# Splitting evacuations from matmuls in a hand-ordered attention and wave-mixing kernel, with a named PSUM bank for each result and a new order of all steps

## The chip, the cores and the metric

The kernel runs on one core of a Trainium2 chip. The metric is device time in microseconds of one execution: the median of three runs. One execution was profiled, and all views of the profile shown here are of that one.

## The reference

Two layers, one after the other, for a batch of 8. The attention of each of 8 heads is a sum of two: full attention among positions pooled by four (576 positions become 144), repeated four times, and a local attention in which a position sees only those less than four away. The second layer takes the result as x (576 rows of 512), makes phases, mixes the rows with two token weights and then the channels.

```
q_d, k_d, v_d = mean of each 4 positions of q, k, v
out_up = repeat(softmax(q_d k_d^T / 8) v_d, 4)
out_local = softmax(where(|i - j| < 4, q k^T / 8, -1e9)) v
x = (out_up + out_local), heads side by side           # 8 x 576 x 512

theta = x @ w_theta
y = w_tok_r @ (x * cos(theta)) + w_tok_i @ (x * sin(theta))
u = x + y
out = u + max(u @ w_ch, 0)
```

Inputs and output are float32; the kernel computes in bfloat16 with float32 sums.

## The kernel before

The work of one batch is cut into steps, and the program is one string, `ORDER`, in which each letter stands for the next step of one kind (a Python generator per letter; batch 0 first, then batch 1, and so on). `pin()` ties every instruction to the one before it on its engine, so the string fixes the order of each engine's queue: an instruction that waits holds up all behind it on that engine. Different engines run as far ahead of one another as data and buffers let them.

The steps of one batch, with their letters before the change:

- L (13 steps): loads on SP's queue into 15 staging buffers of `stg`; eight k and q tiles of two heads each (288 KB), alternating k and q, then five v tiles in two halves. A load waits for the cast of the tile that had its buffer, 15 tiles earlier.
- C (13): casts to bfloat16 into `k_tm`, `q_tm`, `v_w`: POOL, but for batch 0 ACT (k) and DVE (q).
- A (4): nine transposes on PE into a pair of banks (`pstr`, L267), then ACT's copy to `kT` or `qT` (L268).
- a (4): sums of four positions: `kd` on DVE (L281), `qdT` on POOL (L290, L291; batch 0 on DVE, L285).
- U, u: pooled v on PE, ACT's copies, and POOL's products into `vd` (L317).
- P (2): pooled scores in tiles of 64 rows and 128 columns (`psSd`, L339) with ACT's exp; S (3): local scores in blocks of 64 (`psS`, L375) with ACT's exp (L382); M (3): the band mask on DVE.
- N (2): pooled outputs (`psnd`, L403, L409), normalised on DVE; n: their transposes and DVE's copy `xdT`; V (5): local outputs (`psloc`, L447), DVE's reciprocal `rl` and product `tmp`.
- T (5): transposes of `tmp` by matmul, with DVE's sum with the pooled part into `xT` (L480, L485).
- H (5): phases `psth` (L501), ACT's sin and cos into `cs` (L506, L507); the fifth is the tail of 64 rows (`pstt`). h: DVE's product `zT` of the tail and its DMA transpose into row group 8 of `z` (L524, L527). Z (4): transposes of `xT` (L537) and DVE's products `z` (L538).
- X (8): the token mix, nine matmuls of 288 columns each (`psu`, L558) and DVE's sum `uT` (L562). All nine row groups of `z` go into each.
- r (5): four DMA transposes of `uT` into `ur` on SP (L571), and POOL's copy of the tail into `ut`; t: the DMA transpose `utr` of two batches' tails.
- R (4), Q: channels (`psr`, L588; `psrt`); O (4), q: DVE's relu and sum `osb`, `osbt` (L607, L613), which need `ur` or `utr`; o, s: stores on SP.

The weights have letters of their own: l (20 loads: four of `w_theta`, twelve of the token weights, four of `w_ch`), c (20 casts on POOL), and w (18): transposes of the token weights (`wps`, L245) into `WT` (L250), nine for each half of 288 token columns. The token weights are cut into rows of 128, 128 and 32 for each half. D (4) is a group of six matmuls on zeros (`wu`, L160), which stands at the end of the string.

In the transposes, scores and other steps with a result in PSUM, the matmuls and the instruction that takes the result out belong to one step. PSUM banks are handed out in turn: `w1` has four single banks, `w2` two pairs. Before the first step, constants are made: DVE's memsets and copies, with POOL's selects between them (`halves_of`, L89 to L99), in the order of the text. So DVE's first casts of q stand behind all of them.

Of the kernel before, what the change touches and what calls it, by code (L numbers as in the profile page):

```python
# [14 lines left out]

P = 128
B = 8
# [10 lines left out]

# [12 lines left out]
OC = [128, 128, 32, 128, 128, 32]  # L41
OR = [0, 128, 256, 288, 416, 544]
# [3 lines left out]
def kernel(  # L46
# [14 lines left out]
    wpool = ctx.enter_context(tc.tile_pool(name="wpool", bufs=1))  # L61
    stg = ctx.enter_context(tc.tile_pool(name="stg", bufs=15))
    work = ctx.enter_context(tc.tile_pool(name="work", bufs=2))
    moep = ctx.enter_context(tc.tile_pool(name="moep", bufs=2))
    ps2 = ctx.enter_context(tc.tile_pool(name="ps2", bufs=1, space=bass.MemoryType.PSUM))
    ps1 = ctx.enter_context(tc.tile_pool(name="ps1", bufs=1, space=bass.MemoryType.PSUM))

    turn2, turn1 = itertools.cycle("ab"), itertools.cycle("abcd")

    def w2(name, dt=FP32):  # L70
        return ps2.tile([P, 2, 512 if dt == FP32 else 1024], dt, tag="w2" + next(turn2), name=name)

    def w1(name, dt=FP32):
        return ps1.tile([P, 512 if dt == FP32 else 1024], dt, tag="w1" + next(turn1), name=name)

    dve, act, gp = nc.vector.tensor_copy, nc.scalar.copy, nc.gpsimd.tensor_copy
# [3 lines left out]
    ident = const.tile([P, P], BF16, name="ident")  # L80
    nc.vector.memset(ident, 0.0)
    nc.gpsimd.affine_select(out=ident, in_=ident, compare_op=ALU.not_equal, fill=1.0,
                            base=0, pattern=[[-1, P]], channel_multiplier=1)
    identw = ident.rearrange("p (g w) -> p g w", w=W)

    pihc = const.tile([P, 1], FP32, name="pihc")
    nc.vector.memset(pihc, PIH)

    def halves_of(t, n, val, cuts):  # L89


        full = work.tile([P, 2, W], BF16, tag="full", name=f"full_{t.name}")
        nc.vector.memset(full, val)
        for g in range(2):
            for base, col, row in cuts[g]:
                nc.gpsimd.affine_select(out=full[:, g, 0:n], in_=full[:, g, 0:n], compare_op=ALU.is_ge, fill=0.0,  # L96
                                        base=base - W * g * row, pattern=[[col, n]], channel_multiplier=row)
        for g in range(2):
            nc.vector.tensor_copy(out=t[W * g:W * g + W, :], in_=full[W * g:W * g + W, g, 0:n])  # L99

    band = const.tile([P, W], BF16, name="band")
    halves_of(band, W, 1.0, [[(3, -1, 1), (3, 1, -1)]] * 2)


    kTs, kds = [], []
    for i in range(2):
        t = const.tile([P, 4, NCH * CH], BF16, name=f"kT{i}")
        nc.vector.memset(t[:, :, S:], 0.0)
        kTs.append(t)
        t = const.tile([P, 4, NCH, KP], BF16, name=f"kd{i}")  # L110
        nc.vector.memset(t, 0.0)
        kds.append(t)

    v_ws = []
    for i in range(2):
        t = const.tile([P, NCH, H, 66], BF16, name=f"v_w{i}")
        nc.vector.memset(t[:, :, :, 64:65], 1.0)
        v_ws.append(t)

    vds = []  # L120
    for i in range(2):
        t = const.tile([P, 2, H, 66], BF16, name=f"vd{i}")
        nc.vector.memset(t[:, :, :, 64:65], 0.0)
        for c in range(4):
            nc.vector.memset(t[KP * c:KP * c + PG, 0, :, 64:65], 1.0)
            nc.vector.memset(t[KP * c:KP * c + SD - 4 * PG, 1, c::4, 64:65], 1.0)
        vds.append(t)

    PU = []
    for c in (0, 1, 4):
        r = const.tile([P, KP], BF16, name=f"pu{c}")
        cuts = []
        for blk in (2 * c, 2 * c + 1):
            lo, n = W0[blk] - CH * c, STEP * blk - W0[blk]
            cuts.append([(lo, -4, 1), (3 - lo, 4, -1)])
            if n:
                cuts[-1].append((-n, 0, 1))
            if n + OWN[blk] < W:  # L140
                cuts[-1].append((n + OWN[blk] - 1, 0, -1))
        halves_of(r, KP, 0.25, cuts)
        PU.append(r)
    PU = [PU[0], PU[1], PU[1], PU[1], PU[2]]

    own = const.tile([P, 4], BF16, name="own")
    nc.vector.memset(own, 1.0)
    nc.gpsimd.affine_select(out=own, in_=own, compare_op=ALU.is_ge, fill=0.0,
                            base=0, pattern=[[-KP, 4]], channel_multiplier=1)
    nc.gpsimd.affine_select(out=own, in_=own, compare_op=ALU.is_ge, fill=0.0,  # L150
                            base=KP - 1, pattern=[[KP, 4]], channel_multiplier=-1)

    warm = const.tile([P, 512], BF16, name="warm")
    nc.vector.memset(warm, 0.0)

    def warm_up():
        for i in range(WARM):
            ps = w1(f"wu{i}")
            for _ in range(6):
                nc.tensor.matmul(out=ps, lhsT=ident, rhs=warm, start=True, stop=True)  # L160
            yield

    WARM = 4
# [5 lines left out]
    def stage(b, key):  # L169
        t = staged[b, key] = stg.tile([P, S], FP32, tag="st", name=f"st{b}_{key}")  # L170
        return t

    def load(b):
        for hh in range(4):
            for nm, src in (("k", k), ("q", q)):
                nc.sync.dma_start(out=stage(b, f"{nm}{hh}"),
                                  in_=src[b, 2 * hh:2 * hh + 2].rearrange("h (p r) d -> (h p) (r d)", r=WR))
                yield
        for c in range(NCH):
            t = stage(b, f"v{c}")[:, 0:DM].rearrange("p (h d) -> p h d", d=D)  # L180
            for g in range(2):
                lo = W0[2 * c + g]
                nc.sync.dma_start(out=t[W * g:W * g + W], in_=v[b, :, lo:lo + W, :].rearrange("h p d -> p h d"))
            yield

    def cast(b):
        q_tm = work.tile([P, 2, WR, 2, D], BF16, tag="q_tm", name=f"q_tm{b}")
        k_tm = work.tile([P, 2, WR, 2, D], BF16, tag="k_tm", name=f"k_tm{b}")
        v_w = v_ws[b % 2]
        inputs[b] = (q_tm, k_tm, v_w)  # L190
        eng = CASTS.get(b, CASTS[None])
        for hh in range(4):
            for i, (nm, dst) in enumerate((("k", k_tm), ("q", q_tm))):
                eng[i](out=dst[:, hh // 2, :, hh % 2, :],  # L194
                       in_=staged.pop((b, f"{nm}{hh}")).rearrange("p (r d) -> p r d", d=D))
                yield
        for c in range(NCH):
            eng[2](out=v_w[:, c, :, 0:D], in_=staged.pop((b, f"v{c}"))[:, 0:DM].rearrange("p (h d) -> p h d", d=D))  # L198
            yield

    CASTS = {0: (act, dve, gp), None: (gp, gp, gp)}
# [3 lines left out]
    wth = wpool.tile([P, 4, DM], BF16, name="wth")  # L205
    wch = wpool.tile([P, 4, DM], BF16, name="wch")
    WT = wpool.tile([P, 9, S], BF16, name="WT")
    w_tm = [moep.tile([P, 6, S], BF16, tag="uT", name=f"wtm{ri}") for ri in range(2)]

    def wide_weight(w, nm):  # L210
        for i in range(4):
            nc.sync.dma_start(out=stage("w", f"{nm}{i}")[:, 0:DM], in_=w[P * i:P * i + P, :])
            yield

    def weight_loads():
        yield from wide_weight(moe_w_theta, "th")
        for hf in range(2):
            for ri, w in enumerate((moe_w_tok_r, moe_w_tok_i)):
                for ct in range(3 * hf, 3 * hf + 3):
                    nc.sync.dma_start(out=stage("w", f"tok{ri}{ct}")[0:OC[ct]], in_=w[OR[ct]:OR[ct] + OC[ct], :])  # L220
                    yield
        yield from wide_weight(moe_w_ch, "ch")

    def weight_casts():
        for i in range(4):
            gp(out=wth[:, i, :], in_=staged.pop(("w", f"th{i}"))[:, 0:DM])
            yield
        for hf in range(2):
            for ri in range(2):
                for ct in range(3 * hf, 3 * hf + 3):  # L230
                    gp(out=w_tm[ri][0:OC[ct], ct, :], in_=staged.pop(("w", f"tok{ri}{ct}"))[0:OC[ct]])
                    yield
        for i in range(4):
            gp(out=wch[:, i, :], in_=staged.pop(("w", f"ch{i}"))[:, 0:DM])
            yield
# [16 lines left out]

    parts = {}

    def turns(b):
        q_tm, k_tm, v_w = inputs[b]
# [4 lines left out]
        for i in range(2):  # L263
            for n, (tm, To) in enumerate(((k_tm, kT), (q_tm, qT))):
# [6 lines left out]
                )  # L271
                yield

    EVAC = (act, act)

    def sums(b):
        qT, kT, qdT, kd = parts[b]
# [424 lines left out]
```

## Time and profile before

| what | value |
|---|---|
| median of 3 runs | 257.98 us (257.93 to 260.31) |
| profiled execution, span | 258.0 us |
| PE busy | 229.7 us, 89% |
| DVE busy | 196.5 us, 76% |
| ACT, POOL busy | 138.9 us, 54%; 118.0 us, 46% |
| mean granted PE clock | 0.980 |
| DMA | 49.85 MB, 193 GB/s in the mean |
| matmuls | 3332 |

The profiled execution has no time of its own beside its span of 258.0 us, which is the median to 0.02 us. Busy times of a queue are unions of its instructions' spans; a matmul that runs at half clock is busy for twice as long. The page's second part cuts the span in 40 slices of 6.45 us. "Waits" put the idle time before an instruction down to what came last. SP runs no arithmetic: its queue issues the DMAs, and the DMA engines work beside all.

### The profile page before, as it was taken

What the parts mean: (1) busy time and instruction counts of PE and PEld (TensorE: products, weight loads), DVE (VectorE), ACT (ScalarE), POOL (GpSimd) and SP (SyncE); (2) the same over time, 40 slices, a digit from 0 to 9 for tenths busy, and PEclk for the clock granted to TensorE, in tenths of its full rate; (3) what the DMA queues carried; (4) which work ended last, traced back from release to release, by engine and by line L of the source; (5) the groups of instructions that cost most, each with busy time, mean ns of one, the idle gap of its engine ahead of it and who ended that gap; (6) DMA issues with size and microseconds to landing.
All of it is one profiled execution on the core that took longest, in us unless ns stands there. A gap on an engine that the chain in (4) does not pass through costs nothing.

```text
span 258.0 us, 8100 instructions
## 1 busy us (share of the span) xinstructions
PE 229.7 (89%) x3332; PEld 157.8 (61%) x3332; DVE 196.5 (76%) x404; ACT 138.9 (54%) x190; POOL 118.0 (46%) x201
## 2 busy tenths in 40 slices
PE   0168879999999998699998999989899899999998
PEld 0154656588557765377676667766586457677633
DVE  4298797878998965487889698897789987856452
ACT  3456469634985579504894568357775765250000
POOL 3664989464796596449274444941043020000000
PEclk9999999589999999979999999999999999999999
DMA  7999996698998995998699864994088316015756
GB/s 228 265 248 357 344 198 175 197 248 202 285 225 194 287 275 135 208 326 151 129 311 259 156 153 103 326 216 62 3 125 241 90 41 185 12 35 122 205 177 231
DMA packets 83173, 49.85 MB, mean 193 GB/s; under 512 B 68160, under 2 KB 68160, under 8 KB 83136
## 3 DMA queue, kind: packets, MB, share of 16 engines
q1 hardware_dynamic: 83136, 49.33, 77.0%
q8 instruction: 26, 0.43, 0.7%
q14 instruction: 11, 0.09, 0.1%
HBM read 34.11 MB, written 9.44 MB: 169 GB/s over the span
## 4 chain that ended last, share of the span: by engine, by line
PE 63%; DVE 12%; DMA 8%; ACT 6%; POOL 6%; issue 4%; SPq 0%; DVEq 0%; POOLq 0%; ACTq 0%
PE psu L558 25%; PE psr L588 7%; PE psth L501 6%; PE pstr L267 6%; DMA z<-zT 4%; PE xTps L480 3%; DVE tmp L456 2%; DMA st_k<-in_k_dram 2%; DVE xT L485 2%; PE wu L160 2%; PE psS L375 2%; PE psxt L537 2%; POOL full_pu L96 2%; PE psnd L403 2%; PE psloc L447 2%
## 5 line engine op out<-in xcount | busy, mean ns | idle before, releaser
L558 PE MATMUL psu<-WT,z 128*128 128x288 bf16 x576 | 81.1, 292 | 4.9 <-DVE z L538 2.4
L558 PEld LDWEIGHTS <-z 128*128 128x128 bf16 x576 | 55.4, 99 | 22.0 <-DVE z L538 2.7
L562 DVE TENSOR_TENSOR uT<-psu,xT 128x288 bf16<-128x288 f32 x64 | 29.0, 454 | 19.9 <-PE psu L558 19.3
L198 POOL CAST v_w<-st_v 128x512 bf16<-128x512 f32 x40 | 26.1, 664 | 30.3 <-DMA st_v<-in_v_dram 16.1
L506 ACT ACTIVATE cs<-psth,pihc 128x512 bf16<-128x512 f32 x32 | 22.2, 694 | 20.9 <-PE psth L501 16.8
L501 PE MATMUL psth<-wth,xT 128*128 128x512 bf16 x128 | 33.2, 387 | 0.2 <-ACT cs L507 0.2
L588 PE MATMUL psr<-wch,uT 128*128 128x512 bf16 x128 | 31.3, 379 | 1.1 <-DVE osbt L613 0.6
L456 DVE TENSOR_TENSOR tmp<-psloc,rl 128x512 bf16<-128x512 f32 x40 | 27.7, 692 | 1.4
L382 ACT ACTIVATE pm<-psS 128x1024 bf16<-128x1024 f32 (+1 forms) x24 | 20.5, 883 | 14.9 <-PE psS L375 14.7
L268 ACT COPY kT<-pstr 128x1152 bf16<-128x1152 bf16 x16 | 18.0, 1126 | 16.3 <-PE pstr L267 16.1
L538 DVE TENSOR_TENSOR z<-psxt,cs 128x1024 bf16<-128x1024 bf16 x32 | 21.5, 684 | 6.2 <-PE psxt L537 3.8
L573 POOL COPY ut<-uT 128x256 bf16<-128x256 bf16 x8 | 3.2, 400 | 50.2 <-DVE uT L562 50.2
L485 DVE TENSOR_TENSOR xT<-xTps,xdT 128x464 bf16<-128x464 f32 (+1 forms) x40 | 24.7, 629 | 1.0 <-PE xTps L480 0.4
L607 DVE SCALAR_TENSOR_TENSOR osb<-psr,ur 128x512 f32<-128x512 f32 x32 | 21.5, 685 | 5.0 <-DMA ur<-uT 3.5
L194 POOL CAST k_tm<-st_k 128x576 bf16<-128x576 f32 x28 | 19.4, 694 | 5.5 <-DMA st_k<-in_k_dram 5.2
L268 ACT COPY qT<-pstr 128x1152 bf16<-128x1152 bf16 x16 | 18.1, 1133 | 7.0 <-PE pstr L267 7.0
L281 DVE TENSOR_REDUCE kd<-kT 128x290 bf16<-128x1160 bf16 x16 | 21.6, 1353 | 0.0
L194 POOL CAST q_tm<-st_q 128x576 bf16<-128x576 f32 x28 | 18.7, 667 | 5.0 <-DMA st_q<-in_q_dram 4.9
L290 POOL TENSOR_TENSOR two<-qT 128x576 f32<-128x576 bf16 x14 | 16.0, 1146 | 7.9 <-ACT qT L268 7.9
L390 DVE TENSOR_TENSOR pm<-pm,band 128x1024 bf16<-128x1024 bf16 (+1 forms) x24 | 18.9, 787 | 1.0 <-ACT pm L382 1.0
L267 PE MATMUL pstr<-ident,k_tm 128*128 128x128 bf16 x144 | 12.1, 236 | 8.4 <-ACT k_tm L194 7.1
L317 POOL TENSOR_TENSOR vd<-last,own 128x256 bf16<-128x256 bf16 x16 | 10.1, 653 | 20.6 <-ACT last L311 20.6
(83 smaller groups left out, 370.0 us busy)
## 6 DMA issues: line engine op xcount, KB each, us to landing
st_v<-in_v_dram SPq DMA_DIRECT2D x80, 128.0 KB, 4.1
st_k<-in_k_dram SPq DMA_DIRECT2D x32, 288.0 KB, 4.5
st_q<-in_q_dram SPq DMA_DIRECT2D x32, 288.0 KB, 5.0
out_dram<-osb SPq DMA_DIRECT2D x32, 256.0 KB, 3.1
stw_tok<-in_moe_w_tok_r_dram SPq DMA_DIRECT2D x4, 288.0 KB, 6.2
stw_tok<-in_moe_w_tok_i_dram SPq DMA_DIRECT2D x4, 288.0 KB, 5.8
stw_th<-in_moe_w_theta_dram SPq DMA_DIRECT2D x4, 256.0 KB, 5.7
stw_ch<-in_moe_w_ch_dram SPq DMA_DIRECT2D x4, 256.0 KB, 5.8
```

What stands on the lines that cost most here:

```text
L194: eng[i](out=dst[:, hh // 2, :, hh % 2, :], in_=staged.pop((b, f"{nm}{hh}")).rearrange("p (r d) -> p r d", d=D))
L198: eng[2](out=v_w[:, c, :, 0:D], in_=staged.pop((b, f"v{c}"))[:, 0:DM].rearrange("p (h d) -> p h d", d=D))
L267: nc.tensor.transpose(out=ps[:, P * r:P * r + P], in_=tm[:, i, r, :, :], identity=ident)
L268: EVAC[n](out=To[:, 2 * i:2 * i + 2, 0:S].rearrange("p a (w r) -> p a w r", r=WR), in_=ps[:, 0:P * WR].rearrange("p (r a w) -> p a w r", a ...
L281: nc.vector.tensor_reduce(out=kd[:, hs, :, 0:PG].rearrange("p e g m -> p (e g) m"), axis=AX.X, op=ALU.add, in_=kT[:, hs, :].rearrange("p e ...
L456: nc.vector.tensor_tensor(out=tmp.rearrange("p g (j d) -> p g j d", d=D), in0=pv[:, :, :, 0:D], in1=rl.unsqueeze(3).to_broadcast([P, 2, 4, ...
L485: nc.vector.tensor_tensor(out=xT[:, :, CH * c:CH * c + cnt].rearrange("p e (m j) -> p e m j", j=4), in0=ps[:, :, 0:cnt].rearrange("p e (m ...
L501: nc.tensor.matmul(out=th, lhsT=xT[:, dc, P * c:P * c + P], rhs=wth[:, dc, :], start=(dc == 0), stop=(dc == 3),)
L506: nc.scalar.activation(out=cs[:, 0, :], in_=th, func=AF.Sin, bias=pihc, scale=1.0)
L558: nc.tensor.matmul(out=ps[:, 0:288], lhsT=z[:, j, P * dc:P * dc + P], rhs=WT[:, j, cols], start=(j == 0), stop=(j == 8),)
L562: nc.vector.tensor_tensor(out=uT[:, dc, cols], in0=ps[:, 0:288], in1=xT[:, dc, cols], op=ALU.add)
L588: nc.tensor.matmul(out=psr, lhsT=uT[:, dc, P * c:P * c + P], rhs=wch[:, dc, :], start=(dc == 0), stop=(dc == 3),)
```

## The change

It rewrites the kernel around the same arithmetic.

- Each step with a PSUM result is split in two, the matmuls and the evacuation, with letters of their own. Where it matters below: A/a (turns and ACT's copies), S/s/m, P/p, N/n, O/o/i (local outputs, reciprocals, products), T/t, H/h, G/g/Z/z (the tail: phases, sines, DVE's product, DMA transpose on SP), X/y, V/v (weight turns and DVE's copies), J/j (mix and `uT`), R/f/F (DMA transposes of `uT`, the tail's copy, `utr`), K/b, E/r (channels and relu), D, Y (stores), d and e (key and query sums), k (constants), L, C, l, c as before, w (a single warm-up matmul, which does not occur in the new order).
- A second string names the PSUM bank of each result, any of eight; `two()` takes the pair that holds it. Tiles are fixed buffers (`rot`), with the same counts as the pools had.
- The k tiles of one pair of heads are loaded and cast next to each other. Batch 0's casts stay on ACT and DVE.
- The token weights are loaded, cast and transposed in six tiles of 96 rows.
- A pooled score of a head pair is two matmuls of 64x64 instead of one of 64 rows and 128 columns.
- The constants are a sequence among the others; those with selects are made on POOL alone.
- The order is new, and the warm-up matmuls at the end are gone.

```
+    def one(dt=FP32):
+        i = int(next(banks))
+        ap = pairs[i // 2][:, i % 2, :]
+        return ap if dt == FP32 else ap.bitcast(dt)
...
-        full = work.tile([P, 2, W], BF16, tag="full", name=f"full_{t.name}")
-        nc.vector.memset(full, val)
+        full = rot("full", [P, 2, W], BF16, 2)
+        nc.gpsimd.memset(full, val)
...
-            nc.vector.tensor_copy(out=t[W * g:W * g + W, :], in_=full[W * g:W * g + W, g, 0:n])
+            nc.gpsimd.tensor_copy(out=t[W * g:W * g + W, :], in_=full[W * g:W * g + W, g, 0:n])
...
+    ITEMS = ["k0", "k1", "q0", "q1", "k2", "k3", "q2", "q3", "v0", "v1", "v2", "v3", "v4"]
+    CASTS = {0: "aavvaavvppppp", None: "ppppppppppppp"}
...
-OC = [128, 128, 32, 128, 128, 32]
-OR = [0, 128, 256, 288, 416, 544]
+OC = 96
...
-            for par in range(2):
-                nc.tensor.matmul(out=dst(par), lhsT=kd[64 * par:64 * par + 64, hh, 0:4, :],
-                                 rhs=qdT[64 * par:64 * par + 64, hh, :], start=True, stop=True)
+            for m in range(2):
+                for par in range(2):
+                    nc.tensor.matmul(out=dst(par)[64 * m:64 * m + 64], lhsT=kd[64 * par:64 * par + 64, hh, 2 * m:2 * m + 2, :],
+                                     rhs=qdT[64 * par:64 * par + 64, hh, :], start=True, stop=True)
...
     def mix(b):
...
+        z = zs[b]
+        for dc, hf in pieces(b):
+            ps = held["u", b, dc, hf] = one()[:, 0:288]
+            for j in range(9):
+                nc.tensor.matmul(out=ps, lhsT=z[:, j, P * dc:P * dc + P], rhs=WT[:, j, 288 * hf:288 * hf + 288],
+                                 start=(j == 0), stop=(j == 8))
+            yield
+
+    def mix_out(b):
+        xT = xTs[b]
+        uT = uTs[b] = rot("uT", [P, 6, S], BF16, 2)[:, 0:4, :]
+        for dc, hf in pieces(b):
             cols = slice(288 * hf, 288 * hf + 288)
...
+            nc.vector.tensor_tensor(out=uT[:, dc, cols], in0=held.pop(("u", b, dc, hf)), in1=xT[:, dc, cols], op=ALU.add)
...
+    ORDER = (
+        "LLkLkCCACLaCLLLALkCCLllaCLLCkLeAkaAkLLadSLeLLkSdsklkklkCcSLkmlPLCcLCCLssOmmCPUlpOCuoiLpCoLlCCOluxxAl"
+        "iNncNnaCcCCcnoliTALdaAOnCaLAociLQOaqeLStdoTeTtPsltlimPCcHHplXTCLtpcchVOLHcCCoCXvVilvLlhVvXhTVtCLcyUH"
+        "ucvOuyoyVGhvVixvVLxNVlnvgcSNnvSTsnVnLvVvCsZcccAVLLvzVVvVvVCXvTLvyQVValvLqmvCCtAtJaLCLVCOjLJjlmCvLoHO"
+        "iOoLlJoheLTLCiJLCLAcjTLtaCiAtdCHTXCCXaLtLHCHALdheyhaChJcCyXGjJUgjyCjCSRuPZupXzCxlJyjAsLcxaLJRmCLJjLf"
...
+        "soOQqofiJTALCYimALTaJTtCRttHaOjoOLJCXhiTJoXRijCTHyetXejhCHtGUdDhjdJgHKyuuRZyXhSjbPzyPJxsppJmSOjoiJjs"
+        "JOmjOoSjoixsRiJNKTjmDnNRDnnJfnObOKooQiTJDbqtDFRKTtjHTiXtKtTjHthyHHhGEXJgbZKXhXhzbryyyjRKRJjJjJDbJJJY"
+        "RDjJJjjKfKbDjjKRjbfDRRbKDbbDKbFKDDEbrDDY"
+    )
```

## The prediction

> **What bounds the kernel now.** I read the page first, then the windows, the waits of PE and the chain of waits between 84 and 110 us, and priced PE's steps in the timeline.
>
> ```profile
> PE 229.7 (89%) x3332; PEld 157.8 (61%) x3332; DVE 196.5 (76%) x404; ACT 138.9 (54%) x190; POOL 118.0 (46%) x201
> PE   0168879999999998699998999989899899999998
> PEclk9999999589999999979999999999999999999999
> DMA  7999996698998995998699864994088316015756
> ```
>
> PE is the bound, but 89% flatters it: where the clock is halved, half the busy time is no work. So I priced each step by its start-to-start time between 110 and 170 us: a mix group of nine matmuls (X) 1.11, a phase or channel group of four (H, R) 0.865, nine transposes (A) 0.50, a score unit (S) 0.28, an output unit (V) 0.24, a weight turn (w) 0.20. All steps of the program come to 202.3 us. PE's real work runs from 7.08 to 251.96, 244.9 us, so 42.6 us are lost. Counting the steps done per stretch: 20.0 us of work by 50 us, then 8.6, 9.4, 8.8, 9.0, 7.8, 7.2 in each ten up to 110, 8.2 up to 120, and 123 in the 130 us after that. The start loses most; the next hole is 80 to 120.
>
> ```profile
> PE pstr L267 <- ACT k_tm L194: 7.1, 1, 7.1
> PE pstr L267 <- DVE q_tm L194: 6.0, 1, 6.0
> PE psu L558 <- DVE z L538: 2.4, 1, 2.4
> ```
>
> The first two are the start: the first q transposes wait until 14.2 us, because the q casts stand on DVE behind constants that DVE and POOL pass back and forth (DVE's waits have 5.4 us for `pu` and 1.1 us for `band`). The third is at 107 to 110 us, and the chain of waits says how it came about:
>
> ```profile
> 87.19 0.89 POOL k_tm L194
> 88.08 0.99 POOL two L290
> 89.07 5.32 DMA st_k<-in_k_dram
> 94.45 0.67 POOL k_tm L194
> ...
> 98.77 0.68 PE pstr L267 x9
> ...
> 104.11 3.96 DMA ur<-uT
> 108.29 0.69 DVE osb L607
> 108.98 0.61 DVE z L538
> ```
>
> PE has run up to the loads: batch 4 is turned as soon as it is cast. Then `osb` waits on DVE for a transpose DMA, z is queued behind it, and PE stands still.
>
> ```profile
> 45.00:47.50 2.50, 2.26 (x36) 1.71 (x38) 2.50 (x8) 2.10 (x3) 1.67 (x3) 0.73 0.28 59
> 47.50:50.00 2.50, 2.50 (x45) 1.10 (x45) 1.63 (x5) 2.01 (x4) 0.00 (x0) 0.50 0.67 193
> 50.00:52.50 2.50, 2.50 (x41) 1.72 (x38) 1.98 (x5) 0.18 (x2) 2.24 (x4) 0.50 0.98 354
> 52.50:55.00 2.50, 2.50 (x34) 2.21 (x33) 1.95 (x5) 0.00 (x0) 1.44 (x3) 0.91 0.99 317
> ```
>
> Columns behind the window: its length, busy PE, PEld, DVE, ACT, POOL, granted clock, DMA share, GB/s. Two things: the clock is halved around 50 us (0.27, 0.50, 0.50 and 0.09 of 2.5 us lost, 3.4 us), and the DMA share falls to 0.28, because SP stands behind the transpose of `zT` (issued at 45.0) with loads waiting.
>
> **The change, part by part.**
>
> *Constants and first casts.* POOL now builds `band`, `pu` and `own` alone: 29 selects, 6.1 us by their rows, 8 copies and 6 memsets on POOL that the trace does not show in this form, between 0.10 us (POOL's memset of 128x1) and 0.40 (its copy of 128x256) each: 7.5 to 11.7 us in all. They are nearer the small row; and the first v cast, next on POOL, waits for its load until about 12, so I take nothing (at most 0.3). DVE's q casts no longer wait. By the loads' rows (third tile 6.35 us, fifth 7.83, so 0.74 a tile) k0 and k1, now loaded first, are cast by 6.0 instead of 7.0; q0, q1 by 7.9; the fourth A is evacuated at about 13.5 instead of 18.8. But DVE then still has 0.65+0.27+0.65+0.65 us of memsets and 5.4 us of sums before the first mask: 18.3 instead of 20.5.
>
> *The token weights.* This lead does not last. The new letters put rows 10 to 15 of the weight loads between the loads of batch 2, and PE has weight turn 10 (which needs all of them) before the first mix. With 0.74 a k or q tile, 1.83 a v tile (ten halves in 9.15 us), 0.66 and 0.55 a weight tile by bytes, the loads up to that point sum to 47.9 us; the same sum for the old order gives 43.5 for batch 1's last v tile, whose cast began at 44.8, so I take 49. Then its cast 0.66, two casts of batch 2 behind it on POOL (1.3), transposes 0.5 to 1.0: the first mix starts at 52.1, with 22.4 us of PE work done before it. Before, PE had done 22.4 at 54.1. **Minus 2.0**; from minus 4.0 (weights at 47) to plus 2.0 (at 53).
>
> *The loads against PE.* The new order turns later: before the first A of batch 4 stand 67.9 us of PE work (was 57.1), of batch 5 91.0 (was 78.8). The cover of 10.8 us is more than the 5.3 us DMA of the chain above; and the load queue meets `z` of batch 0 seven tiles later. So the hole of 80 to 110 goes: 30 us for 24.1 of work, against 1.8 lost in the 20 us before, so 5.9 - 2.7 = 3.2 us; and with it the half clock behind it (0.65 over 109.6 to 114.2, 1.6, with its edge 1.7). **Minus 4.9**; between 0 and minus 7. What is late next is `ur` of batch 0: its fourth transpose now stands on SP behind batch 4's sixth load. Summing SP's issue rows (v tile 1.8, others 0.4, transposes 1.25) it is issued at about 82 and, with the 2.3 to 7.0 us to landing (median 3.9), done at 84 to 89; DVE reaches `osb` of batch 0 at about 84. **Plus 1.0**, between 0 and the 3.5 us that the same wait cost before.
>
> *Evacuations and banks.* No instruction is added: DVE's sum of rows is 209.3 us in both orders, and ACT goes from 18 to 16 changes between exp and sin, 2.6 us on an engine at 54%. The waits of PE on banks are 0.9 us or less each now. Nothing, minus 2 to plus 3, since every engine's order is new.
>
> *Pooled scores.* 64 matmuls more. A 64x64 unit shows 32 matmuls in 0.28 us, so four run at once; the old group took 0.35 for eight. Nothing if they do; 0.35 times 8, 2.8 us, if they don't. I take nothing: the nearest row has the same tile. *Weights of 96 rows*: 12 casts at 0.66 for 8 at 0.66 and 4 at 0.66. Nothing.
>
> *The end.* The 24 warm-up matmuls go; they ended at 257.1, but the last store, issued by 254.2, lands at about 257 too. After the last mix the new order has 6.1 us of PE work (6.9 before) and the tail's transpose last: `utr` lands some 7.0 us after, four `osb` and `osbt` end at 8.5, two stores 1.1 and 2.4 to land. That is 12.0 and 0.8 of closing, against 13.75 before; but one channel group (0.865) moved ahead of that point. Nothing, plus or minus 1.
>
> The sum is made on the profiled execution, span 258.0, beside a median of 257.98: 258.0 - 2.0 - 4.9 + 1.0 = **252.1 us**.
>
> **The rivals.**
>
> *The residual DMA holds DVE (slower).* For: `ur` stands behind more loads than before, and what waits behind `osb` on DVE (rl, tmp, uT, z) feeds PE at once. Against: it happened once in the old run, and later batches have fewer loads in front. Each time costs what it cost at 106 to 109.6 us, 3.6 of standstill and 1.7 of half clock, 5.3. Twice decides: 258.0 - 2.0 - 4.9 + 10.6 = **261.7**; three times 267.0.
>
> *The weights come later and PE cools.* The loads of batch 1 and 2 are behind by 2 us, and the wait ahead of weight turn 10 is one more stretch of 3.4 us at half clock: minus 2.0 becomes plus 1.7, and the rest stays: **255.8**. For it: PE has nothing else to do there. The change then does only half of what it says.
>
> *The clock stays up.* The trace shows 0.50 right behind a stretch in which PE was busy 2.50 of 2.50 us, most of it weight turns. If it is these in a row that count as rest, spreading ten of them among phases and outputs keeps the clock, and the 3.4 us at 45 to 55 are saved: **248.7**. Against it: a wait for the weights comes right there. The Trainium skill, page TensorE: Matmul & The Clock Gate, section Part 4: PE-mode transpose, says that transposes do not count as busy for the clock in the same way; the trace agrees, with 0.50 after them. By Part 1 of that page of the Trainium skill an idle window of about 3.4 us halves the clock too, which speaks against this rival.
>
> **How the numbers follow.** Forecast 0.46, the cool weights 0.16, the clock 0.12, the residual 0.24, and 0.02 for faster ways still. Faster by over 1% (about what a measurement can tell from no change: below 255.4) is the forecast, the clock and the 0.02: 0.60. Within 1%: 0.16. Slower: 0.24. The forecast's own range is 248 to 256; with cases of both signs the range runs from 246 (every gain at its far end but one) to 262, which leaves out three residual waits.
>
> **What would show it.** Right: the first q transposes at about 8 us; the first mix at about 52, after a wait of PE on POOL's weight casts; no load on the chain between 80 and 110; clock 1.0 at 110; the last chain through `utr` and stores. Wrong: waits of several us of `osb` on `ur`, PE below 9 us of 10 between 60 and 120, or DVE as the releaser of PE in the second half.

## The result, and the profile after

| | before | after |
|---|---|---|
| median | 259.14 us, 4 runs (257.93 to 260.42) | 325.55 us, 4 runs (321.65 to 328.05) |
| span of the profiled execution | 258.0 us | 323.3 us |
| PE busy; idle (span less busy) | 229.7; 28.3 us | 239.8; 83.5 us |

The ratio is 1.252, 95% interval 1.239 to 1.265: a quarter slower, where 252.1 us was forecast. Medians here and below are of all runs, while ratios and their intervals leave out runs more than 1.5% above the fastest of the same kernel. First the page's lines, as shown of before:

```profile
PE 239.8 (74%) x3344; PEld 162.8 (50%) x3372; DVE 192.4 (60%) x390; ACT 137.4 (43%) x188; POOL 119.5 (37%) x215
PE   1656975759588897887689587878987888757853
PEclk9999999598699999997999989999999999997977
DMA  7999996597049998999158838471433032213263
```

Every engine but PE is busy for about as long as before. PE has more busy time only because more of it is at half clock (busy time times granted clock, summed over the span, is 224.5 us before and 225.3 after); its idle time tripled. And there is no hole to point at: between the first slice and the last, PE stands at 5 to 9 tenths, also in the last quarter, where the DMA share is 0 to 6 tenths and loads can hardly be the limit. What is lost is lost a little at each step.

The waits say at which (engine, line, who it waited for: us in total, times, longest). Three lines of PE's list:

```profile
PE pair L665 <- DVE osb L678: 6.7, 4, 3.6
PE pair L630 <- ACT cs L561: 6.1, 2, 4.0
PE pair L553 <- DVE uT L639: 4.5, 3, 3.1
```

and four of DVE's, the first of them the longest in its list:

```profile
DVE uT L639 <- PE pair L630: 24.6, 18, 4.0
DVE uT L639 <- PE pair L665: 9.0, 3, 6.5
DVE uT L639 <- PE pair L605: 4.3, 1, 4.3
DVE uT L639 <- PE pair L526: 3.9, 2, 3.6
```

The first line of DVE is a sum that waits for its own mix, as before the change (19.3 us in 29 places). By the arithmetic none of the others has to be. The channels (L665) use no `osb`, the mix (L630) no `cs` and the phases (L553) no `uT`; the sum `uT` (L639) takes out the mix, not the channels (L665), the turned x (L605) or the transposed outputs (L526). A result waits for other results. A matmul may have to wait for the evacuation of an older result whose bank it takes; for an evacuation that waits for the matmuls of another result there is no such reason. One place in the timeline of the changed kernel shows how (start, length, engine, line, what, and in brackets the idle time before it and who ended it):

```profile
83.81 0.64 ACT L561 ACTIVATE cs<-pair 128x512 bf16<-128x512 f32 x1
84.49 2.32 PE L630 MATMUL pair<-WT,z 128*128 128x288 bf16 x9 [3.96 <-ACT cs L561]
...
86.61 0.63 PE L605 MATMUL pair<-ident,xT 128*128 128x128 bf16 x4
...
87.34 0.46 DVE L639 TENSOR_TENSOR uT<-pair,xT 128x288 bf16<-128x288 f32 x1 [4.26 <-PE pair L605]
...
90.07 0.23 PE L336 MATMUL pair<-v_w,pu 128*32 128x128 bf16 x4
...
90.43 0.46 DVE L639 TENSOR_TENSOR uT<-pair,xT 128x288 bf16<-128x288 f32 x1 [2.63 <-PE pair L336]
```

Put the string of banks beside it. The mix at 84.49 is the fifth of batch 0, in bank 6. It starts when ACT has read the fourth phases of batch 1 (83.81 and 0.64), which lie in bank 7. It is done at 86.81, and its sum is the one at 90.43: that waits for the pooled v of batch 2, which is written into bank 7 until 90.30. The sum at 87.34 takes out bank 2, and waits for the turned x in bank 3. Banks 6 and 7 are one tile of the program, `pairs[3]`, and 2 and 3 are `pairs[1]`. The program's own list of waits (the semaphores that each instruction waits for) has all three: this mix waits for the semaphore that ACT raises after that `cs`, its sum for the last matmul of the pooled v, and the sum at 87.34 for the turned x. Meanwhile PE idled 3.96 us and its clock fell: the 2.32 us for nine matmuls are twice the usual 1.1.

### The profile page after: what moved, and what is told of

It reads as the page before. It is cut to its first block, busy times and chain, and to the rows that moved or that the text cites. A ratio compares the mean times of both kernels' runs of the same rounds, so it can differ in the third digit from the quotient of the medians.

```text
span 323.3 us, 8176 instructions
## 1 busy us (share of the span) xinstructions
PE 239.8 (74%) x3344; PEld 162.8 (50%) x3372; DVE 192.4 (60%) x390; ACT 137.4 (43%) x188; POOL 119.5 (37%) x215
## 5 line engine op out<-in xcount | busy, mean ns | idle before, releaser
L630 PE MATMUL pair<-WT,z 128*128 128x288 bf16 x576 | 85.6, 300 | 13.6 <-ACT cs L561 6.1
L630 PEld LDWEIGHTS <-z 128*128 128x128 bf16 x576 | 56.9, 102 | 33.0 <-issue 14.9
L639 DVE TENSOR_TENSOR uT<-pair,xT 128x288 bf16<-128x288 f32 x64 | 28.1, 450 | 46.5 <-PE pair L630 24.6
L665 PE MATMUL pair<-wch,uT 128*128 128x512 bf16 x113 | 34.0, 410 | 11.9 <-DVE osb L678 6.7
L553 PE MATMUL pair<-wth,xT 128*128 128x512 bf16 x116 | 33.0, 404 | 12.5 <-DVE uT L639 4.5
L678 DVE SCALAR_TENSOR_TENSOR osb<-pair,ur 128x512 f32<-128x512 f32 x32 | 21.6, 685 | 24.9 <-ACT cs L561 6.4
L538 DVE TENSOR_TENSOR xT<-pair,xdT 128x464 bf16<-128x464 f32 (+1 forms) x40 | 24.5, 632 | 17.5 <-PE pair L526 5.7
L218 POOL CAST v_w<-st 128x512 bf16<-128x512 f32 x40 | 24.8, 639 | 21.1 <-DMA st<-in_v_dram 20.6
L560 ACT ACTIVATE cs<-pair,pihc 128x512 bf16<-128x512 f32 x32 | 22.1, 692 | 21.8 <-PE pair L553 8.0
L506 DVE TENSOR_TENSOR tmp<-pair,rl 128x512 bf16<-128x512 f32 x40 | 27.1, 684 | 0.7
L610 DVE TENSOR_TENSOR z<-pair,cs 128x1024 bf16<-128x1024 bf16 x32 | 21.6, 682 | 9.3 <-ACT cs L561 3.8
L553 PEld LDWEIGHTS <-xT 128*128 128x128 bf16 x128 | 12.1, 102 | 24.7 <-issue 13.5
L665 PEld LDWEIGHTS <-uT 128*128 128x128 bf16 x128 | 12.5, 102 | 24.0 <-issue 14.9
```

Source lines behind the costliest of these rows:

```text
L218: copies[e](out=v_w[:, c, :, 0:D], in_=staged.pop((b, it))[:, 0:DM].rearrange("p (h d) -> p h d", d=D))
L506: nc.vector.tensor_tensor(out=tmp.rearrange("p g (j d) -> p g j d", d=D), in0=held.pop(("loc", b, c))[:, :, :, 0:D], in1=rls.pop((b, c)).u ...
L538: nc.vector.tensor_tensor(out=xT[:, :, CH * c:CH * c + cnt].rearrange("p e (m j) -> p e m j", j=4), in0=held.pop(("xT", b, c))[:, :, 0:cnt ...
L553: nc.tensor.matmul(out=th, lhsT=xT[:, dc, P * c:P * c + P], rhs=wth[:, dc, :], start=(dc == 0), stop=(dc == 3))
L560: nc.scalar.activation(out=cs[:, 0, :], in_=th, func=AF.Sin, bias=pihc, scale=1.0)
L610: nc.vector.tensor_tensor(out=z_of(b)[:, 2 * c:2 * c + 2, :], in0=held.pop(("xt", b, c)).unsqueeze(1).to_broadcast([P, 2, DM]), in1=css.po ...
```

## The experiments

**Theory:** two banks that lie in one tile are held as one. A matmul into either waits until whatever stood in the other is taken out, and an evacuation of either waits for the matmuls that were issued into the other. **Rival:** the new order is slow by itself, or the constant tiles (`rot`, fixed buffers) are.

**Sharing alone, on the kernel before.** Its four single banks become two tiles of two banks; as a control, four fixed tiles of one bank.

```
+    shared = [ps1.tile([P, 2, 512], FP32, tag=f"sh{i}", name=f"sh{i}") for i in range(2)]
 ...
-        return ps1.tile([P, 512 if dt == FP32 else 1024], dt, tag="w1" + next(turn1), name=name)
+        i = "abcd".index(next(turn1))
+        ap = shared[i // 2][:, i % 2, :]        # control: shared[i][:, :], four tiles of [P, 512]
+        return ap if dt == FP32 else ap.bitcast(dt)
```

> The kernel before, in its own order, with its four single banks as two fixed tiles of two banks each, and nothing else changed. T1: clearly slower, 275 to 310, since neighbouring results now wait for each other. T2: 257 to 262, as before.

> The control of the one before: the kernel before with its four single banks as four fixed tiles of one bank each instead of tiles out of a rotating pool. T1 and T2: 257 to 262. If it is slow, fixed tiles are the cost, and not that two banks share one.

Measured: 363.22 us, 1.399 of before (1.393 to 1.406), and the control 259.64, 1.000 (0.998 to 1.003). Same order, same instructions, same eight banks: a tile boundary is worth 104 us. The loss is larger than expected; that neighbours in the rotation are the results most often alive together would explain it, but wasn't measured. DVE's waits with shared tiles:

```profile
DVE uT L566 <- PE sh L562: 57.8, 47, 4.5
DVE z L542 <- PE sh L541: 27.8, 19, 3.9
```

and in the control:

```profile
DVE uT L566 <- PE sh L562: 20.9, 28, 4.7
DVE z L542 <- PE sh L541: 5.7, 6, 3.1
```

These lines name only themselves: DVE waits for its own matmuls, which come late. Why they come late stands in PE's list with shared tiles:

```profile
PE sh L541 <- ACT cs L511: 12.0, 8, 2.6
PE sh L562 <- ACT cs L511: 7.4, 4, 2.6
```

Neither the transposes of x (L541) nor the mix (L562) uses `cs`, and in the control no wait of PE for another result's evacuation is above 0.9 us in total. The pair of runs shows that the tile is the reason.

**How near the partner is.** The same two tiles, but banks a and c, b and d together: `ap = shared[i % 2][:, i // 2, :]`.

> The kernel before with its four single banks in two tiles of two banks, as in the run that took 363.2 us, but the two banks of a tile are those that are used two results apart (a with c, b with d) instead of next to each other (a with b, c with d). If the loss comes from results that are alive at the same time in one tile, each result still has a partner: the matmuls into it have to wait until the partner, two results older, is taken out, which is what a rotation through two banks instead of four would cost. The partner is further away, so less than before: 300 to 350 us. If only the number of tiles counts, 363 again; if neighbours alone hurt, under 270.

310.15 us in two runs, 1.195 (1.186 to 1.204): as expected between. The same tiles with partners one result further apart lose half as much (51 us). That fits a price that goes with how often both halves are in use at once; how often they are was not counted.

**Separating the banks in the changed kernel.** Eight tiles of one bank, with order and bank string kept. A result of two banks is then in two tiles and is taken out by two instructions (184 more), so the kernel before was run with the same splits.

```
-    pairs = [psum.tile([P, 2, 512], FP32, name=f"pair{i}") for i in range(4)]
+    singles = [psum.tile([P, 512], FP32, name=f"bank{i}") for i in range(8)]
 ...
-            nc.vector.reciprocal(out=rl, in_=held["loc", b, c][:, :, :, 64])
+            for g in range(2):
+                nc.vector.reciprocal(out=rl[:, g, :], in_=held["loc", b, c][g][:, :, 64])
```

> The changed kernel with each of the eight banks as a tile of its own; a result over two banks is taken out by two instructions, one for each bank, instead of one. Order, bank string and matmuls stay. Theory T1 (two banks that share a tile are held as one by the framework's dependencies, so a matmul into one bank waits for the evacuation of the other, and an evacuation for matmuls into the other): the time falls from 325 to 270 or less, and DVE's waits on PE results of other kinds go. Rival T2 (the new order itself, or waits in it that follow from the true data, is slow): 310 or more, also since 72 ACT and 112 DVE instructions are added.

> The kernel before with the same splitting of its evacuations over two banks: the price of splitting alone. T1 and T2: 258 to 268 (DVE gets some 112 instructions of 0.1 to 0.2 us more, on an engine at 76%).

261.0 us, 1.004 of before (0.998 to 1.009), against 325.55; and the kernel before with the splits 261.69, 1.007 (1.005 to 1.010). So the tiles were the whole loss against the kernel before, and the splits cost some 2 us in the old order. With both split, old and new order differ by 0.7 us, which these intervals can't tell from nothing. In PE's list no line that waits for another result is above 1.1 us now; what it names first are its inputs:

```profile
PE bank L285 <- ACT k_tm L220: 5.3, 2, 5.1
PE bank L636 <- DMA z<-zT: 4.0, 2, 2.5
PE bank L367 <- DVE kd L302: 3.2, 2, 2.8
```

In the program's list of waits, the sum of the fifth mix of batch 0 now waits only for the last matmul of its own mix. This settles the cause: the order and the constant tiles (`rot`) are those of the changed kernel, so neither rival is left. It leaves a second question: the forecast gain of 5.9 us is not there either. The other runs look for it.

**Three parts without the order.** The kernel before with constants on POOL alone, weight rows of 96 and pooled scores of 64x64.

> The kernel before, in its old order and with its old banks, with three parts of the change: the constants band, pu and own (and the zeros of the identity) made by POOL alone, token weights in six rows of 96, pooled scores in 64x64 tiles. The prediction gives these nothing each; the q casts of batch 0 leave DVE's constants behind and the first q transposes come some 2 to 5 us earlier. Theory one: PE then waits for the loads instead, 258.5 to 260.5 us beside 259.5. Rival: the earlier start is kept to the end, 255 to 258. Against both: 64x64 pooled scores cost 0.35 us a batch more, 2.8 in all, 262.

260.76 us, 1.006 (1.001 to 1.010): just past theory one's range, and short of the 262 at which the pooled scores would cost what was feared. The start is earlier and does not last. Busy time by stretch (length, PE, PEld, DVE, ACT, POOL, granted clock, DMA share, GB/s), first before, then with the parts:

```profile
0.00:20.00 20.00, 5.61 (x100) 4.86 (x101) 11.38 (x48) 8.78 (x10) 10.57 (x40) 1.00 0.90 249
40.00:60.00 20.00, 19.76 (x320) 14.66 (x319) 15.74 (x38) 12.72 (x17) 13.24 (x21) 0.83 0.75 201
```

```profile
0.00:20.00 20.00, 8.29 (x148) 5.70 (x148) 11.44 (x38) 12.16 (x15) 12.61 (x53) 1.00 0.97 254
40.00:60.00 20.00, 16.86 (x254) 12.05 (x257) 13.49 (x34) 10.06 (x12) 14.56 (x21) 0.83 0.93 226
```

2.7 us of PE won in the first 20 us are 2.9 lost between 40 and 60, while the DMA share is 0.93.

**The late weights.** The changed kernel with eight tiles, and token weight rows 10 to 15 loaded ahead of the first six loads of batch 2 (`LlllLLlLlLLl` becomes `llllllLLLLLL` at the same places of the order).

> The changed kernel with each bank its own tile (261.0 us), and the loads of token weight rows 10 to 15 moved ahead of the six loads of batch 2 among which they stood; nothing else. In that kernel the last two weight casts waited 1.2 and 2.3 us for their loads and the first mix came at 57.3 us where 52.1 was predicted. If the late weights are what ate the predicted 2.0 us, the last of them lands some 3 us earlier, the first mix comes at 53 to 55 and the time is 257.5 to 260. Rival: PE has other work to do there or batch 2 is then late by as much, so the mix comes earlier and the end does not: 260.5 to 262.

264.06 us, 1.014 (1.006 to 1.023): past the rival's own figure. Beside the 1.004 (0.998 to 1.009) of the eight tiles alone the intervals overlap, so it is not shown to be slower than that, but nothing is won. The first mix came at 56.8 instead of 57.1 us, and a wait for batch 2 came in (POOL, in this kernel):

```profile
46.57 0.67 POOL L220 CAST k_tm<-st 128x576 bf16<-128x576 f32 x1 [4.77 <-DMA st<-in_k_dram]
```

**Cheaper loads.** The v loads read rows of 2 KB instead of pieces of 256 bytes, the same bytes in all, in the kernel before and in the changed one with eight tiles. The values of v are then in other places than the reference's, so these runs only price the loads.

```
-  in_=v[b, :, lo:lo + W, :].rearrange("h p d -> p h d")
+  in_=v[b].rearrange("h p d -> (h p d)")[DM * lo:DM * (lo + W)].rearrange("(p h d) -> p h d", h=H, d=D)
```

> The kernel before, with the v loads taken from 64 rows of 2 KB that lie one behind the other instead of 64 x 8 pieces of 256 bytes: the same number of bytes, tiles, issues and casts, but the values of v are in the wrong places, so the output is not the reference's. It takes the transfers' share of time down and leaves everything else. Theory: loads set the pace of the first 110 us (a v tile took 1.83 us of the queue, a k or q tile 0.74 with more bytes; the DMA share is 0.9 to 1.1 in most stretches to 120 us), and no order of the same loads can bring the 4.9 us of the hole at 80 to 110 back. Then the time falls by at least 4.9 us, 245 to 253. Rival: the order of the work and the waits between engines made the hole, and the loads are only the last link: 256 to 259.5.

> The changed kernel with each bank its own tile (261.0 us), with the same wide v loads and so with values of v in the wrong places. If loads set the pace of the first 110 us it falls by as much as the kernel before does with them or more, since in the new order PE has its work earlier: 246 to 254. If the new order's own waits (the casts of the token weights, osb for ur) hold it, 257 to 261.

256.51 us, 0.988 (0.981 to 0.995), and 256.45, 0.980 (0.969 to 0.991). The first lies on the rival's side: loads are part of it, but not the 4.9 us. The lever was also shorter than I took it for: 36,000 fewer packets lowered the transfers' share of the span only from 77.0 to 73.9%. In the new order the same edit brought 4.6 us between the medians, and the result lies between the two expected ranges. Its ratio rests on two runs of 252.84 and 255.72 us, and the transfers' share stayed (75.0 and 75.2%); that more hangs on the loads in the new order is not shown.

**Transposes on another queue.** All DMA transposes issued by ACT, and only those of `zT` (`nc.scalar.dma_start_transpose`).

> The kernel before, with the transposes by DMA (z of a batch's tail, the four ur of a batch, utr) issued by ACT instead of SP, at the same places of the order. They then no longer stand behind loads that wait for a staging tile, and loads no longer stand behind transposes that wait for zT or uT. If that queue is what made osb wait 3.5 us for ur and the DMA share fall to 0.28 around 47 us, 254 to 257 us. Rival: some 44 issues of 1.25 us each, 55 us, and their waits for uT stand on ACT ahead of exponentials and sines that PE and DVE wait for; ACT is busy 139 of 258 us, so it would come to 75% with waits on top: 262 to 285 us.

> The kernel before, with only the eight transposes of zT issued by ACT instead of SP. SP waited 27.8 us in five places at that line, 10.1 in one, with loads behind it and the DMA share at 0.28; ACT comes to the same place only after its own sines for that zT, and waits there for one product on DVE. Theory: the loads move up, 254 to 258.5. Rival: the eight issues of about 1.25 us with the wait for DVE, some 2 us each, stand ahead of ACT's exponentials and cost PE as much as they bring, as all 44 transposes did: 259.5 to 264.

275.61 us, 1.059 (1.051 to 1.066), and 271.2, 1.046 (1.039 to 1.052): the first inside its rival's range, the second beyond it, for eight issues of 1.2 us. The loads did not come free of z: in the kernel before SP waited 27.8 us in five places at the transposes of z, and with z on ACT it waits for them still. The longest waits of SP's queue there:

```profile
SPq L571 <- DMA z<-zT: 30.3, 5, 10.4
SPq L176 <- DMA z<-zT: 9.7, 1, 9.7
```

The program's own list of waits tells the two lines apart (place on its engine, line, transfer, semaphores):

```
ACT 35 L527 DmaTransposeAnt z0_604<-zT_0_904 128x4x128 [waits DMAHW5_49,DVE_49]
SP  53 L176 DMACopy st2_k0_886<-in_k_dram 128x576 [waits DMAHW5_49,Pool_49]
ACT 61 L527 DmaTransposeAnt z1_1514<-zT_1_1682 128x4x128 [waits DMAHW3_49,DMAHW2_49,DMAHW5_49,DMAHW0_49,DVE_49]
```

Transfers of both queues take turns at eight semaphores, and each waits for the one that had its semaphore last: the load of batch 2 for the transpose of z on the other queue. The transposes wait besides for the transposes issued before them on the other queue, in both directions: that is L571's 30.3 us, which the expectation of the last run below put to the turns. The Trainium skill, page DMA: Bandwidth & Descriptors, section Silent corruption: two transposing streams in flight at once, says that a transposing stream has to wait for the full completion of the other's; this trace has that wait, 30.3 us of SP's queue. How much of the 12 us it makes, and how much the new waits on ACT's own queue (up to 4.0 us before an issue) make, was not separated.

**Loads ahead of the transposes.** At z of batches 0, 1 and 2 the four loads behind it on SP go ahead (`h` of the order moves past four `L` or `l`).

> The kernel before with one edit of its order: at the transposes of zT of batches 0, 1 and 2, the four loads that stand behind the transpose on SP are put ahead of it. In the run with z on ACT, SP's loads waited 9.7 us for z's transpose though it stood in another queue, and SP's ur for it 30.3 us in five places: a transfer waits for the one that stands eight places ahead, whichever queue it is in. Only the order of the transfers themselves can then keep a late one from holding the loads. In the kernel before SP waited from 41.2 to 45.0 us with some seven of fifteen staging tiles taken and the DMA share fell to 0.28. Theory: four loads of 0.74 us fill that gap, up to 3 us of loads come earlier, of which wide v loads showed that about 2.9 us could be had in all: 257 to 259. Rival: z lands later by what the loads take, PE waits for it in the first mix, and nothing is won: 259 to 261.

265.09 us, 1.023 (1.018 to 1.028): the rival's mechanism, well past its figure. PE waited 7.7 us for z in three places, where it had waited 1.6 in two. Around batch 0 the loads did fill the gap (DMA share 0.87 and 1.63 where it was 0.43 and 0.28). At batch 2 `zT` was ready at 106.8, its transpose was issued behind the loads at 111.34, and landed 5.27 us later:

```profile
112.30 0.66 PE L558 MATMUL psu<-WT,z 128*128 128x288 bf16 x2 [2.08 <-DVE z L538]
116.66 2.58 PE L558 MATMUL psu<-WT,z 128*128 128x288 bf16 x10 [3.70 <-DMA z<-zT]
```

The first of these waits stood in the kernel before too (2.4 us, behind `osb`); the second is the price of the four loads.

With the v loads as they have to be, no version was faster than the kernel before.

## Why the prediction was wrong

- **"Evacuations and banks. ... Nothing, minus 2 to plus 3"** is the step that failed. It asked how many instructions are added and how long PE waits on banks now, in a program whose singles are tiles of their own. The diff had the answer on one line: `ap = pairs[i // 2][:, i % 2, :]`, a view of half a tile. What had to be priced was not the bank a result has but the tile it shares, and with whom. It is the 65 us, and no rival had it. The wait was in nobody's row before, because before no two results shared a tile; the bound "plus 3" came from waits that a different structure had made. The prediction's signs of being wrong did come: PE was busy 31.64 of 40 us between 80 and 120, and DVE stands among its releasers.
- **The start.** Right as told, for what it was worth: the first q transposes came at 8.2 us (8.4 with eight tiles; predicted about 8, before 14.2). That "this lead does not last" was right too, as the run of the parts shows.
- **The token weights, minus 2.0.** Mis-sized. With eight tiles the first mix came at 57.1 us, not 52.1; the last weight tile's cast waited until 52.9 where the sum of loads took 49:

```profile
52.92 0.67 POOL L246 CAST uT<-st 96x576 bf16<-96x576 f32 x1 [2.25 <-DMA st<-in_moe_w_tok_i_dram]
```

  The sum of prices per tile takes each transfer for as long as the mean of a row: a q tile of batch 1 was in flight from 22.41 to 31.96, 9.55 us, where the median is 5.2, and between 30 and 40 us PE was busy 6.05 of 10 at a clock of 0.51. The mechanism of the rival "the weights come later and PE cools" is there with its size: PE stood 2.55 us for POOL's weight casts until 53.65, and the clock was 0.50 from 54.1 to 57.5, 3.4 us. The longer stretch at 30 us was in no rival. Loading the weights earlier made batch 2 wait instead.
- **The loads against PE, minus 4.9.** Not found. Between 80 and 120 us PE was busy 36.03 us with eight tiles and 35.64 before, and the half clock is there in both, for 3.4 us each (from 108.7 and from 111.0). The hole has another last link, the transpose of z (the chain has it from 104.43 to 109.13 us).
- **`osb` waiting for `ur`, plus 1.0.** Too small: 8.8 us in five waits on DVE with eight tiles, 3.5 in one before. This was the rival of the residual DMA, and its wait is there. That 261.0 lies near its 261.7 is luck: the rival keeps the 4.9 and the 2.0 as won, and neither was.
- **Pooled scores, rows of 96, constants: nothing each.** Held within 1%: 1.006 for the three together.
- **The rival "the clock stays up"** rested on half clock behind weight turns at 50 us. In the control with fixed tiles, with the same order and time, that stretch ran at 1.00, weight turns and all; its half clock was at 97 to 105 us. So it does not come with that step in every execution. Nor is it worth the 3.4 us: in 20 runs of the kernel before the mean clock was 1.00, with a median of 258.8 us; in 13 it was 0.993, with 260.3, and in 14 between 0.967 and 0.987, with 259.7.
- **The range** took its ends from rows of the old structure. With the tiles apart 261.0 would have been inside it, near the upper end, which is no merit of its terms.
- **The base of the sum** mixed two measures. The span of 258.0 is not the median "to 0.02 us": in every run on record the time is 1.7 to 2.1 us longer than the span (260.88 and 259.2 with eight tiles). A span of 252.1 would have been a time of about 253.8.

What stays open: how the gap between the forecast and the 261.0 us with eight tiles divides between the loads, the transposes and the splits. The new order with two-bank results taken out whole and singles apart wasn't tried: its results need up to eight singles or four pairs, out of the same eight banks.

## What to carry to other kernels

Before pricing a change of buffers, write down for each result which tile (not which bank or bytes) it lives in and what else lives there at the same time: dependencies were kept by the tile here, and two independent results in one tile became one chain through three engines, worth 65 us in one kernel and 104 in another. When every stretch of a profile gets evenly slower and instructions keep their lengths, look in the waits for an instruction that waits for a line whose result it doesn't use. And two DMA queues share more than they seem to: here a transfer that was moved to another queue still took its turn at the same eight semaphores.

## What the runs showed of the hardware

- Nothing in these runs made the two banks wait in hardware: the same eight banks, with the same bank for each result and the same order of steps, ran in 261.0 us once each was a tile of its own. The Trainium skill, page PSUM — Partial Sum Buffer, section PSUM bank collisions raise a hardware error, gives bank and quadrant as the unit to guard; the program guarded two banks. A collision itself is in no run here.
- A gap cost PE more than its length, and the clock kept a beat of its own. In the last run, around the waits of 2.08 and 3.70 us (columns as above):

```profile
110.00:112.50 2.50, 0.42 (x3) 0.13 (x2) 1.54 (x3) 0.30 (x1) 2.42 (x4) 0.94 0.95 293
112.50:115.00 2.50, 0.46 (x2) 0.00 (x0) 1.15 (x3) 0.00 (x0) 1.85 (x4) 0.50 1.16 320
117.50:120.00 2.50, 2.50 (x19) 1.81 (x18) 0.60 (x2) 0.00 (x0) 2.16 (x4) 0.50 1.18 322
120.00:122.50 2.50, 2.50 (x12) 1.61 (x11) 2.27 (x4) 0.00 (x0) 0.68 (x2) 0.51 0.72 125
```

  In narrower windows the clock fell at 112.2, 2.0 us after PE had stopped, and came back at 122.5, after 5.8 us of full work at 0.50. The Trainium skill, page TensorE: Matmul & The Clock Gate, section Part 1, has half clock after an idle window of about 3.4 us and full clock after as long a busy one, and calls the window free-running. The trace agrees with the length and the free running: all changes of this run, at 81.5, 84.9, 112.2 and 122.5, lie whole multiples of 3.41 us apart. It differs in the idle window: the 3.41 us that ended at 112.2 had PE busy for 1.4 of them.
